# Two attention layers on one core: the first loads of a kernel, dealt differently to two DMA queues

## The chip, the cores and the metric

The kernel runs on one core of a Trainium2 chip. A core has a matrix engine (TensorE, PE in the profile), three engines for element-wise work (VectorE = DVE, ScalarE = ACT, GpSimd = POOL), a queue engine without arithmetic (SyncE = SP) and 16 DMA engines that move data between main memory (HBM) and the core's own memory (SBUF). A load is an instruction on one engine, here SP or ACT; that engine is busy with it while the load is issued ("SPq", "ACTq" in the profile), and the data arrives later ("to landing"). The metric is device time in microseconds (us), the median of several runs.

## The reference

Two independent problems A and B with the same shapes (all bf16) are computed and put side by side:

```python
B, Sq, D = 16, 32, 1024
Hq, Hkv, Sk, Dh = 32, 4, 512, 128
q = (x @ wq).reshape(B, Sq, Hq, Dh).transpose(0, 2, 1, 3)
k = repeat(k_cache, Hq // Hkv, axis=1); v = repeat(v_cache, Hq // Hkv, axis=1)
p = softmax(einsum("bhqd,bhkd->bhqk", q, k) * Dh ** -0.5)
o = einsum("bhqk,bhkd->bhqd", p, v)
out = o.transpose(0, 2, 1, 3).reshape(B, Sq, Hq * Dh) @ wo
result = concatenate([out_A, out_B], axis=-1)
```

For each problem x is 512 tokens by 1024 features, wq is 1024 by 4096 (32 heads of 128 columns), wo is 4096 by 1024.

## The kernel before, in words

Everything runs on one core in an order written out by hand: the function `fast_path` records instructions engine by engine, and each engine executes its own list in that order. Three kinds of TensorE work are woven together in one long loop (from line 613 on): scores and values of the attention, one group of 8 heads and 32 tokens at a time, and between them "units" of the big projections (q = x @ wq, then out = o @ wo), one matmul each. Later loads are tied to slots of that loop.

The change concerns what comes before the loop: the first eight heads of q of problem A (lines 455 to 556). A matmul contracts 128 features, so x and wq are cut along their 1024 features into eight chunks, numbered from 0. For a chunk TensorE needs x transposed (features on the partitions, the tile `xT[0]`) and the rows of wq for that chunk (the tiles `w0`). All of it arrives by loads:

- **x plain**, `load_x` (line 465): columns of chunks 0 and 1 only, in two halves of 256 tokens, called x first half and x second half here, 128 KB each. TensorE transposes them itself (`transpose_x`, line 521), eight 128x128 transposes; VectorE copies chunk 0 from PSUM to `xT[0]`, ScalarE copies chunk 1 (line 525).
- **x transposed by the DMA**, `load_x_transposed` (line 468): two chunks in each call, 256 KB, straight into `xT[0]`. Three calls: chunks 2 and 3 (**T2** here), chunks 4 and 5 (**T4**), chunks 6 and 7 (**T6**).
- **wq**, `load_w0` (line 474): chunk 0 for heads 0 to 2 and for heads 3 to 5 (**W0a**, **W0b**, 96 KB each), chunks 1, 2, 3 for heads 0 to 5 (**W1**, **W2**, **W3**, 192 KB each), then heads 6 and 7 of chunks 0 to 3 together (**WR**, 256 KB), chunk 4 (**W4**, 256 KB), chunks 5 and 6 (**W56**, 512 KB) and chunk 7 (**W7**, 256 KB), each for all eight heads.

TensorE's order in this stage is: 22 warm-up matmuls on a constant (line 513); the eight transposes, first half of the tokens, then second half; chunk 0 for heads 0 to 2 in two halves of 256 columns (six matmuls) and for heads 3 to 5 in full width (three); chunks 1, 2 and 3 for heads 0 to 5 (six matmuls each); heads 6 and 7 for chunks 0 to 3 (eight); chunks 4, 5, 6 for all heads (eight each); chunk 7 (eight). These are the 67 matmuls of line 531 in the profile. Then the units of line 301 follow with the next heads.

ScalarE's list starts with its loads and, after the first of them, the loading of the activation table (line 480), ahead of the two copies of line 525.

One more rule sets the order. The loads issued by SP and ACT share eight semaphores that are handed out in turn. The ninth of these loads may be issued only when the first has landed, the tenth when the second has landed, and so on. In the kernel before, the ninth load is WR and the first is x second half.

Of the kernel before, what the change touches and what calls it, by code (L numbers as in the profile page):

```python
# [181 lines left out]
def kernel(  # L182
# [14 lines left out]
    nc = tc.nc  # L197
# [5 lines left out]
    TT = NTOK // P  # L203
# [14 lines left out]
    def fast_path(ok_i):  # L218
        with ExitStack() as fctx:
# [235 lines left out]
            NF = REP - 2  # L455
# [8 lines left out]
            def load_x(t0, t1, eng=nc.sync):  # L464
                eng.dma_start(out=x_sb[:, t0:t1, :], in_=x_v[:, t0:t1, 0:2 * P])  # L465

            def load_x_transposed(d0):
                nc.sync.dma_start_transpose(  # L468
                    out=xT[0][:, d0:d0 + 2, :],
                    in_=A_x.flatten_outer_dims()[:, d0 * P:(d0 + 2) * P],  # L470
                )

            def load_w0(d0, d1, h0, h1, eng=nc.sync):
                eng.dma_start(  # L474
                    out=w0[d0 // HC][:, d0 % HC:(d1 - 1) % HC + 1, h0 * DH:h1 * DH],
                    in_=wq_v[:, d0:d1, h0 * DH:h1 * DH],
                )

            load_x(TT // 2, TT, nc.scalar)
            nc.scalar.preload_act_table_set("natural_log_exp_and_others")  # L480
            load_x(0, TT // 2)
            load_w0(0, 1, 0, NF // 2)
            load_w0(0, 1, NF // 2, NF, nc.scalar)
            load_w0(1, 2, 0, NF)
            load_w0(2, 3, 0, NF, nc.scalar)
            load_x_transposed(2)
            load_w0(3, 4, 0, NF)
            load_w0(0, HC, NF, REP)
            load_w0(HC, HC + 1, 0, REP)
            load_x_transposed(HC)  # L490
            load_w0(HC + 1, DC - 1, 0, REP)
            load_x_transposed(HC + 2)
            load_w0(DC - 1, DC, 0, REP)
            load_wq(0, 2, 0, 2)
# [173 lines left out]
    ok_i = flag.tile([1, 1], I32, name="ok_i")  # L668
    total = 2 * 2 * NG * QW
    ok = fast_path(ok_i)  # L670
    with tc.If(ok < total, preferred_fallthrough_block=True, label="general"):
        general_path(tc, problems, out_flat)
# [30 lines left out]
```

## Time and profile before

| | |
|---|---|
| time, median of 6 runs | 343.07 us (342.67 to 343.26) |
| the profiled execution | 343.47 us, of which the span of the core 341.7 us |
| busy, share of the span | PE 99%, DVE 78%, ACT 54%, POOL 14% |
| matmuls of line 531 (this stage) | 67, mean 376 ns, 14.6 us busy |
| loads of T2, T4, T6 on SP | 3, 1.57, 1.56 and 3.22 us to issue |

Spans are counted from the first instruction of the core. Matmuls are pipelined: the profile's duration of one (379 ns for 512 columns) is from start to modelled end, and two neighbours overlap; what one costs in a dense row is the distance of the starts. A busy share of 99% thus says that TensorE hardly ever had nothing in flight. DMA share in the table of stretches is the mean busy share of the 16 DMA engines; packets in flight at once on one engine can take it above 1.

### The profile page before, as it was taken

The numbers are of one execution on the slowest core, as the hardware profiler recorded it, in microseconds if no ns is written. First come the engines' busy times: TensorE is split into PE (matmuls) and PEld (weight loads), VectorE is DVE, ScalarE is ACT, GpSimd is POOL, SyncE is SP. The second block draws the span as 40 slices with busy tenths as digits, with TensorE's granted clock in tenths as the row PEclk, the third lists the DMA queues.
The fourth block names the chain that finished last, engine by engine and source line by source line (L and its number), as shares of the span: only waits on it lengthen the run. The fifth ranks groups of instructions, "written<-read, shape, count | busy, mean of one in ns | idle before, by whom it ended". The sixth has DMA issues, their size and how long they took to land.

```text
span 341.7 us, 5475 instructions
## 1 busy us (share of the span) xinstructions
PE 337.0 (99%) x2113; PEld 213.0 (62%) x2113; DVE 265.1 (78%) x335; ACT 185.4 (54%) x208; POOL 46.7 (14%) x206
## 2 busy tenths in 40 slices
PE   8999999999999999999999999999999999999996
PEld 5455666666666666666666666666666666666555
DVE  0046988888888888888888988879888888889540
ACT  2058666676667667666645555555555555555110
POOL 0001110011111111110012211222122101111100
PEclk9999999999999999999999999999999999999999
DMA  7999999999999998899999955998449996440001
GB/s 189 280 207 271 296 239 225 211 235 260 307 257 151 231 223 230 206 288 305 324 276 279 272 125 145 336 283 220 118 103 296 358 204 158 106 100 10 17 19 33
DMA packets 128622, 71.70 MB, mean 210 GB/s; under 512 B 76880, under 2 KB 127824, under 8 KB 128592
## 3 DMA queue, kind: packets, MB, share of 16 engines
q1 hardware_dynamic: 127504, 69.78, 83.7%
q0 software_dynamic: 384, 1.05, 0.8%
q10 hardware_dynamic: 704, 0.49, 0.4%
q8 instruction: 17, 0.28, 0.3%
q14 instruction: 13, 0.11, 0.1%
HBM read 50.59 MB, written 2.10 MB: 154 GB/s over the span
## 4 chain that ended last, share of the span: by engine, by line
PE 96%; DMA 2%; SPq 1%; ACT 0%; issue 0%; ACTq 0%
PE f_ps L320 32%; PE q_ps L301 28%; PE ob L425 16%; PE s_ps L357 16%; PE q_ps L531 3%; DMA w_sb<-in_A_wq_dram 2%; SPq L468 0%; SPq L474 0%; SPq L465 0%; ACT o_sb L329 0%; ACTq L329 0%
## 5 line engine op out<-in xcount | busy, mean ns | idle before, releaser
L365 ACT ACTIVATE p_sb<-s_ps,shift 128x1024 bf16<-128x1024 f32 x128 | 142.7, 1115 | 97.5 <-PE s_ps L357 90.1
L376 DVE TRANSPOSE_TENSOR_REDUCE parts<-p_sb 128x32 f32<-128x1024 bf16 x128 | 158.7, 1240 | 21.0 <-ACT p_sb L365 19.3
L320 PE MATMUL f_ps<-wo_sb,oT 128*128 128x512 bf16 (+1 forms) x544 | 132.3, 366 | 0.0
L301 PE MATMUL q_ps<-xT,wq_sb 128*128 128x512 bf16 x448 | 116.9, 379 | 0.0
L425 PE MATMUL ob<-p_sb,v_sb 128*128 128x256 bf16 x512 | 76.8, 273 | 0.0
L357 PE MATMUL s_ps<-qT,kT 128*128 128x256 bf16 x512 | 76.8, 273 | 0.0
L320 PEld LDWEIGHTS <-oT 128*128 128x128 bf16 x544 | 53.2, 98 | 35.3
L357 PEld LDWEIGHTS <-kT 128*128 128x128 bf16 x512 | 56.9, 113 | 28.3
L301 PEld LDWEIGHTS <-wq_sb 128*128 128x128 bf16 x448 | 43.8, 98 | 32.2
L425 PEld LDWEIGHTS <-v_sb 128*128 128x128 bf16 x512 | 50.1, 98 | 20.0
L447 DVE TENSOR_TENSOR oT<-r,ob 128x512 bf16<-128x512 f32 x64 | 43.9, 686 | 19.9 <-PE ob L425 19.4
L411 DVE STREAM_TRANSPOSE r<-rall 128x512 f32<-128x512 f32 x64 | 44.2, 691 | 1.1
L309 ACT CAST qT<-q_ps 128x512 bf16<-128x512 f32 x56 | 32.7, 583 | 16.5 <-PE q_ps L301 16.5
L394 POOL COPY half<-cs 64x32 f32<-64x32 f32 x32 | 6.5, 204 | 232.3 <-DVE cs L384 232.2
L329 ACT CAST o_sb<-f_ps 128x512 bf16<-128x512 f32 (+1 forms) x17 | 9.5, 559 | 23.6 <-PE f_ps L320 23.6
L531 PE MATMUL q_ps<-xT,w_sb 128*128 128x512 bf16 (+1 forms) x67 | 14.6, 376 | 0.7 <-DMA w_sb<-in_A_wq_dram 0.6
L553 DVE CAST qT<-q_ps 128x512 bf16<-128x512 f32 x4 | 2.5, 684 | 13.7 <-PE q_ps L531 13.7
L384 DVE TENSOR_REDUCE cs<-parts 128x32 f32<-128x128 f32 x32 | 12.1, 377 | 1.1
L406 DVE RECIPROCAL rall<-sums 128x32 f32<-128x32 f32 x32 | 10.2, 319 | 3.3 <-POOL sums L403 3.3
L531 PEld LDWEIGHTS <-w_sb 128*128 128x128 bf16 x67 | 6.6, 101 | 8.3 <-DMA w_sb<-in_A_wq_dram 1.6
L553 ACT CAST qT<-q_ps 128x512 bf16<-128x512 f32 x4 | 2.1, 599 | 13.2 <-PE q_ps L531 13.2
L331 POOL DMA_DIRECT2D out_dram<-o_sb x8 | 4.6, 574 | 29.3 <-ACT o_sb L329 29.3
(25 smaller groups left out, 48.2 us busy)
## 6 DMA issues: line engine op xcount, KB each, us to landing
v_sb<-in_A_v_cache_dram SPq DMA_DIRECT2D x16, 512.0 KB, 5.8
wq_sb<-in_B_wq_dram SPq DMA_DIRECT2D x8, 1024.0 KB, 5.9
wo_sb<-in_A_wo_dram SPq DMA_DIRECT2D x8, 1024.0 KB, 7.5
v_sb<-in_B_v_cache_dram SPq DMA_DIRECT2D x16, 512.0 KB, 4.4
wo_sb<-in_B_wo_dram SPq DMA_DIRECT2D x8, 1024.0 KB, 8.5
wq_sb<-in_A_wq_dram SPq DMA_DIRECT2D x5, 1024.0 KB, 6.7
wq_sb<-in_A_wq_dram SPq DMA_DIRECT2D x2, 512.0 KB, 6.7
kT<-in_A_k_cache_dram SPq DMA_TRANSPOSE x64, 4.4
```

The lines of the kernel that those rows point to most:

```text
L301: nc.tensor.matmul(ps[:], lhsT=w[:, dc, (h % 4) * DH:(h % 4 + 1) * DH], rhs=xT[pr][:, dc, :], start=(dc == 0), stop=(dc == DC - 1),)
L309: nc.scalar.copy(out=qT[pr, g][:, :, hl, :], in_=ps[:].rearrange("p (b s) -> p b s", s=SQ),)
L320: nc.tensor.matmul(ps[:, 0:width], lhsT=oT[pr, tt][:, h, :], rhs=wo_tiles[pr, nh, h // REP][:, h % REP, off:off + width], start=(h == 0), ...
L357: nc.tensor.matmul(s_ps[:, c, :], lhsT=kT[:, i % GRP, c, :], rhs=qT[pr, g][:, b, :, :].rearrange("p h s -> p (h s)"), start=True, stop=True,)
L365: nc.scalar.activation(out=p_sb[:], in_=s_ps[:], func=ACTF.Exp, bias=shift[:], scale=SCALE)
L376: nc.vector.tensor_reduce(out=parts[k][:, q, :, :].rearrange("p c h -> p (c h)"), in_=st[i]["p"][:].rearrange("p c (h s) -> p (c h) s", s=SQ),
L384: nc.vector.tensor_reduce(out=cs[:], in_=parts.pop(k)[:].rearrange("p q c h -> p q h c"), axis=AX.X, op=ALU.add,)
L406: nc.vector.reciprocal(out=rall[:, k, :], in_=quad.pop(k)[:])
L411: nc.vector.transpose(out=r[:].rearrange("p n s -> p (n s)"), in_=rall[:, k, o * 2 * REP:(o + 1) * 2 * REP] .unsqueeze(2).to_broadcast([P, ...
L425: nc.tensor.matmul(ob[j][:, q, :], lhsT=v_sb[:, i % GRP, c, :], rhs=st[i]["p"][:, c, :], start=(c == 0), stop=(c == KC - 1),)
L447: nc.vector.tensor_tensor(out=out, in0=rcp.pop(j)[:].rearrange("p (q h) s -> p q h s", h=REP), in1=ob.pop(j)[:].rearrange("p q (h s) -> p ...
L531: nc.tensor.matmul(first_q[h][:, ts], lhsT=w0[dc // HC][:, dc % HC, h * DH:(h + 1) * DH], rhs=xT[0][:, dc, ts], start=(dc == 0 and t0 == 0 ...
```

## The change

T2 goes from SP's list to ACT's, and to the very front of it; it is ACT's only load at the start. The three loads that ACT issued before (x second half, W0b, W2) go to SP. SP's order is now x first half, x second half, W0a, W0b, W1, W2, W3, WR, W4, T4, W56, T6, W7; in the kernel before it was x first half, W0a, W1, T2, W3, WR, W4, T4, W56, T6, W7. What is loaded, in what pieces and into which tiles stays, and so does the work of every other engine. The ninth load is again WR; the first, whose landing it waits for, is now T2.

```diff
-            def load_x_transposed(d0):
-                nc.sync.dma_start_transpose(
+            def load_x_transposed(d0, eng=nc.sync):
+                eng.dma_start_transpose(
                     out=xT[0][:, d0:d0 + 2, :],
                     in_=A_x.flatten_outer_dims()[:, d0 * P:(d0 + 2) * P],
                 )
...
-            load_x(TT // 2, TT, nc.scalar)
+            load_x_transposed(2, nc.scalar)
             nc.scalar.preload_act_table_set("natural_log_exp_and_others")
             load_x(0, TT // 2)
+            load_x(TT // 2, TT)
             load_w0(0, 1, 0, NF // 2)
-            load_w0(0, 1, NF // 2, NF, nc.scalar)
+            load_w0(0, 1, NF // 2, NF)
             load_w0(1, 2, 0, NF)
-            load_w0(2, 3, 0, NF, nc.scalar)
-            load_x_transposed(2)
+            load_w0(2, 3, 0, NF)
             load_w0(3, 4, 0, NF)
             load_w0(0, HC, NF, REP)
             load_w0(HC, HC + 1, 0, REP)
```

## The prediction

> **What bounds the kernel now.** I read the chain of work that ended last, then TensorE's own waits, then TensorE's rows at the start.
>
> ```profile
> PE 96%; DMA 2%; SPq 1%; ACT 0%; issue 0%; ACTq 0%
> PE q_ps L513 <- PEq L687: 0.9, 1, 0.9
> PE q_ps L531 <- DMA w_sb<-in_A_wq_dram: 0.6, 1, 0.6
> ```
>
> The chain is TensorE nearly throughout, and TensorE waited for only two things: the program's start and one load of wq. Behind the first stage it is never idle, so what this stage gains or loses reaches the end one for one.
>
> ```profile
> 3.37 1.06 PE L521 MATMUL xT_ps<-ident,x_sb 128*128 128x128 bf16 x8
> 4.22 0.81 PE L531 MATMUL q_ps<-xT,w_sb 128*128 128x256 bf16 x3
> 5.62 0.38 PE L531 MATMUL q_ps<-xT,w_sb 128*128 128x512 bf16 x1
> 6.55 0.82 PE L531 MATMUL q_ps<-xT,w_sb 128*128 128x512 bf16 x3 [0.55 <-DMA w_sb<-in_A_wq_dram]
> 8.94 3.90 PE L531 MATMUL q_ps<-xT,w_sb 128*128 128x512 bf16 x16
> 19.36 3.62 PE L301 MATMUL q_ps<-xT,wq_sb 128*128 128x512 bf16 x16
> 22.81 0.60 PE L357 MATMUL s_ps<-qT,kT 128*128 128x256 bf16 x4
> ```
>
> The pace of a dense row is (22.81 - 19.36) / 16 = 0.216 us for 512 columns. The last matmul of chunk 0 starts at 5.62, so chunk 1 could start at 5.835; it starts at 6.55, when W1 is there: **0.72 us lost**. The last matmul of chunk 2 starts at 8.94, chunk 3 could follow at 9.15; the chain has W3 landing at 9.38 and chunk 3 from 9.42: **0.27 us lost**. Together 0.99 us, all that this stage loses to late loads of wq.
>
> ```profile
> 3.84 5.54 DMA w_sb<-in_A_wq_dram
> 9.42 10.10 PE q_ps L531 x46
> ```
>
> Why W3 needs 5.5 us where W0a needed 2.8 is seen in the stretches; the last two columns are the DMA engines' busy share and GB/s:
>
> ```profile
> 3.00:3.50 0.50, 0.50 (x7) 0.32 (x5) 0.00 (x0) 0.00 (x0) 0.00 (x0) 1.00 1.06 346
> 5.00:5.50 0.50, 0.50 (x6) 0.36 (x4) 0.00 (x0) 0.00 (x0) 0.00 (x0) 1.00 1.60 278
> 5.50:6.00 0.50, 0.50 (x3) 0.00 (x1) 0.00 (x0) 0.00 (x0) 0.00 (x0) 1.00 1.34 120
> 6.00:6.50 0.50, 0.00 (x0) 0.00 (x0) 0.00 (x0) 0.00 (x0) 0.00 (x0) 1.00 0.62 86
> ```
>
> Between 5.5 and 6.5 the engines are occupied and move about 100 GB/s. That is where T2 (issued 2.22, landing 7.6) is in flight, with W3 behind it in SP's queue and W1 and W2 still running on two queues. The same sag (57 and 20 GB/s) comes at 9.5 to 10.5, when T4 is in flight. [...]
>
> **The change part by part.**
>
> SP's issues. Removed: T2, 1.57 us. Added: x second half (0.46 on ACT), W0b and W2 (0.45 each), 1.36 us. With some 0.05 us between issues SP reaches x first half at 0.74 as before, x second half at 1.25 (ACT had it at 0.82), W0a at 1.75 (1.25), W0b at 2.24 (ACT 1.34), W1 at 2.74 (1.75), W2 at 3.22 (ACT 1.83), W3 at 3.72 (3.84), WR at about 4.3 (4.46).
>
> ACT. T2 is issued at 0.82 instead of 2.22. Taken at SP's 1.57 us it ends at 2.4; the table load (1.28) then ends at 3.7, before the copies of line 525, which started at 4.01. Cost nothing; the cover is 0.3 us. Should the issue take T6's 3.22 us, table and two copies (0.82) end at 6.15, still before 6.55.
>
> x second half. It landed at 0.82 + 3.0 = 3.82. The load issued at 1.25 before, W0a, took 2.8: low end 4.05, 0.23 late. High end: all of T2 passes first; 256 KB at the 250 GB/s or so of the stretches from 2.0 on are 1.0 us: 5.05. T2's first data cannot come much earlier than x's own, so I take a share of a quarter, **4.3**. Transposes and copy took 0.40 to the first matmul of chunk 0 (3.82 to 4.22): chunk 0 starts at 4.7, 0.48 late. W0a at 1.75 + 2.8 = 4.55 is in time; W0b at 2.24 + 2.9 = 5.1 is needed 0.4 to 0.6 after the start, in time or 0.1 late. Three matmuls of 256 columns took 0.213 each at the start (4.22 to 4.86), the next three 0.109: TensorE doubles its pace at about 4.85. A later start puts two of the three behind that point, which returns 0.21. Chunk 0 ends 0.27 late, at **6.10**.
>
> W1. By bytes: x, T2, W0 and W1 are 896 KB; from 2.0 to 5.0 the trace moved 256 GB/s, so 3.6 us from the first data at about 1.75, and some 0.5 to the semaphore: 5.85, inside 6.10. The low end is 2.74 + 2.8 = 5.5, the high end its old 4.8 us, 7.5. I take the bytes, since the 4.8 contains the sag. Chunk 1 starts at 6.10: **0.45 gained** (ends: 0.7 gained, 0.95 lost).
>
> T2 and W3. Chunk 2 needs T2 at 6.10 + 1.30 = 7.4. T2's landing lies between 4.7 us (the first half of problem B's x, 512 KB, in a calmer stretch) and 6.4 (T4, T6): 5.5 to 7.2. In time. W3, with no transposing load ahead of it in its queue, lands by bytes (1280 KB at 256 GB/s) at 7.4, needed at 8.7: **0.27 gained** (ends 0 and 0.27).
>
> SP's ninth load. WR now waits for T2, so SP stands from 4.3 to about 5.5, and WR, W4, T4, W56, T6, W7 and the wq and K loads behind them are issued 1.1 us later. WR is needed at 6.10 + 18 x 0.216 = 10.0 and lands by 5.5 + 4.3: covered, at the rate of W7. T4 would be issued at 6.6, is needed at 11.72, and took 6.4 with the long queue of before, 4.7 with a short one: 11.3 to 13.0. I take it as just in time, because W1 to W3 are through by then. Ends: 0, or 1.3 lost. Behind it, the next wq half landed at 17.2 against a need at 19.4, covered.
>
> Sum: 0.45 + 0.27 = **0.72 us**. The profiled execution (343.47, span 341.7) would become 342.75; it lies 0.40 over the median of 343.07, so the forecast is **342.35**.
>
> [...] The trace shows SP's and ACT's first issues overlapping (0.74 and 0.82) at 0.45 and 0.46 us, no longer than alone. [...]
>
> **The rivals.**
>
> A. *Early loads late.* T2 and x share the DMA engines from the first packet, and T2 holds x second half and W0 back by the full 1.0 us. For it: the sags whenever a transposing load meets others. Against: T2 now meets little unfinished work. Chunk 0 starts at 5.45, ends at 6.75 (1.30 at full pace): 0.20 lost, 0.27 gained, 343.0. Between 342.8 and 343.4.
>
> B. *SP's new wait.* WR behind T2, then T4 late, at chunk 4. For it: T4 landed at 11.9 against a need at 12.45, only 0.57 to spare. Against: the shorter queue. At T4's old 6.4 us it lands at 13.0: 1.3 lost minus 0.72, 343.6. It turns to a net loss once T4 lands after 12.45.
>
> C. *The pace* (the one clearly slower). TensorE's doubling at 4.85 followed unbroken work since 0.93. With x late it stands empty for some 0.5 us between 3.24 and 4.7. If the wait of 3.9 us (0.93 to 4.85) began anew at 4.3, the doubling would come at 8.2: 3.35 us at half pace cost 1.68, minus 0.72, 344.0. It decides when the doubling is over 1.44 us late. Against: the gap of 0.72 us at 5.84 did not slow the matmuls after it. [...]
>
> **How the numbers follow.** Likeliest case 0.55, own range 341.95 to 342.75; A 0.22; B 0.11; C 0.12. 0.2% is 0.69 us, about what a measurement of this kernel tells from no change; the likeliest case sits on that line. Faster: 0.40 + 0.02 + 0.01 = 0.43. Same: 0.15 + 0.17 + 0.03 = 0.35. Slower: 0.03 + 0.07 + 0.12 = 0.22. The range reaches from all 0.99 us gained and a little noise (342.0) to most of B and half of C, 343.8.
>
> **What would show it.** Right: chunk 1 starting at 5.9 to 6.3, chunk 3 without a wait, no sag before 7 us, an unbroken row from there. Wrong: first transposes of the second half after 4.6 (A), a wait of line 531 at chunk 4 (B), 0.43 us between starts of 512-column matmuls after 5 us (C).

## The result, and the profile after

The changed kernel takes **344.90 us** (median of 20 runs, 343.03 to 345.78) against 343.17 (40 runs, 342.67 to 343.62): **0.44% slower, ratio 1.0044 with a 95% interval of 1.0034 to 1.0055**. The ratio weighs all runs; the medians lie 0.50% apart. It was forecast at 342.35.

The median hides the shape. The runs of the changed kernel fall into two groups: 5 of 20 between 343.03 and 343.25, 15 between 344.44 and 345.78, none in between. The kernel before has one group, 0.95 us wide. The profiled execution belongs to the short group: 343.24 us, span 341.3. First the chain by engine and TensorE's waits in it:

```profile
PE 98%; DMA 1%; SPq 0%; ACT 0%; issue 0%; ACTq 0%
PE q_ps L513 <- PEq L687: 0.9, 1, 0.9
PE xT_ps L521 <- DMA x_sb<-in_A_x_dram: 0.6, 1, 0.6
```

The wait for wq in line 531 has gone, as forecast; a new one stands in its place, in the transposes of line 521, for the second half of x. The timeline of the same execution:

```profile
0.82 1.35 ACTq L468 DMA_TRANSPOSE xT<-in_A_x_dram  x1
3.24 0.63 PE L521 MATMUL xT_ps<-ident,x_sb 128*128 128x128 bf16 x4
4.47 0.44 PE L521 MATMUL xT_ps<-ident,x_sb 128*128 128x128 bf16 x4 [0.60 <-DMA x_sb<-in_A_x_dram]
5.05 14.12 PE L531 MATMUL q_ps<-xT,w_sb 128*128 128x256 bf16 x67
19.01 3.62 PE L301 MATMUL q_ps<-xT,wq_sb 128*128 128x512 bf16 x16
```

The first four transposes are through at 3.67, the other four begin at 4.47: TensorE is empty for 0.80 us by starts. From 5.05 on all 67 matmuls follow without a wait worth naming, and line 301 starts at 19.01, 0.35 us earlier than before. So this execution gained, half of what was forecast. The chain runs through W0a, which lands at 5.00:

```profile
1.75 3.25 DMA w_sb<-in_A_wq_dram
```

The landings of the first loads (KB, us from issue) and the stretches (last three columns: granted clock, DMA share, GB/s):

```profile
x_sb<-in_A_x_dram SPq DMA_DIRECT2D x1, 128.0 KB, 2.4
x_sb<-in_A_x_dram SPq DMA_DIRECT2D x1, 128.0 KB, 3.2
xT<-in_A_x_dram ACTq DMA_TRANSPOSE x1, 3.9
...
4.00:4.50 0.50, 0.03 (x1) 0.03 (x2) 0.00 (x0) 0.28 (x1) 0.00 (x0) 1.00 1.35 211
5.50:6.00 0.50, 0.50 (x5) 0.21 (x3) 0.00 (x0) 0.00 (x0) 0.00 (x0) 1.00 1.04 323
6.00:6.50 0.50, 0.50 (x4) 0.20 (x3) 0.00 (x0) 0.00 (x0) 0.00 (x0) 1.00 0.91 314
```

The sag at 5.5 to 6.5 (120 and 86 GB/s before) is gone, the engines move over 300 GB/s there. T2 lands at 4.7 instead of 7.6. The second half of x lands at 4.45 instead of 3.82. None of this explains 344.9; a profile of a long execution does.

### The profile page after: what moved, and what is told of

Its sections match the earlier page's. It is cut to its first block, busy times and chain, and to the rows that moved or that the text cites. A ratio compares the mean times of both kernels' runs of the same rounds, so it can differ in the third digit from the quotient of the medians.

```text
span 341.3 us, 5475 instructions
## 1 busy us (share of the span) xinstructions
PE 336.6 (99%) x2113; PEld 212.8 (62%) x2113; DVE 265.1 (78%) x335; ACT 185.2 (54%) x208; POOL 46.6 (14%) x206
## 4 chain that ended last, share of the span: by engine, by line
PE 98%; DMA 1%; SPq 0%; ACT 0%; issue 0%; ACTq 0%
PE f_ps L320 32%; PE q_ps L301 28%; PE s_ps L357 16%; PE ob L425 16%; PE q_ps L531 4%; DMA w_sb<-in_A_wq_dram 1%; SPq L465 0%; ACT o_sb L329 0%; ACTq L329 0%
```

## The experiments

Two theories stood against each other. **P (pace):** TensorE starts at half pace and doubles it after a stretch of work (256-column matmuls start 0.213 us apart up to 4.86 in the profile of the kernel before, then 0.109); an empty stretch in the first 5 us puts the doubling off. **L (loads):** in long executions loads come still later than in the profile at hand, and TensorE waits for them.

In the table each ratio is to runs of the kernel before from the same series and weighs all runs; it is not the quotient of two medians.

| run | time, us (runs) | ratio to before, 95% interval |
|---|---|---|
| after_again | 345.22 (4; 344.80 to 345.66) | 1.0065 (1.0050 to 1.0079) |
| fill | 343.30 (11; 343.00 to 344.12) | 1.0009 (1.0000 to 1.0018) |
| fill16 | 343.78 (11; 343.05 to 344.61) | 1.0018 (1.0008 to 1.0027) |
| before_w14 | 343.45 (10; 342.72 to 344.83) | 1.0012 (1.0001 to 1.0024) |
| before_x2late | 346.57 (4; 345.99 to 347.38) | 1.0093 (1.0078 to 1.0109) |
| t2_on_sp | 343.63 (10; 343.16 to 344.08) | 1.0014 (1.0005 to 1.0023) |
| x2_then_t2 | 343.83 (12; 343.11 to 346.15) | 1.0035 (1.0018 to 1.0051) |
| table_then_t2 | 344.93 (12; 343.26 to 345.65) | 1.0044 (1.0028 to 1.0061) |
| w3_then_t2 | 343.73 (11; 343.31 to 344.25) | 1.0016 (1.0007 to 1.0025) |
| before_again | 342.57 (1) | |

### The changed kernel again: a long execution

No edit. (The expectation counts 14 long and 6 short runs; of the 20 runs it is 15 and 5.)

> The changed kernel once more, to see an execution of the longer kind (344.4 to 345.8 us, 14 of 20 runs; the other 6 were 343.0 to 343.3). Theory P (pace): TensorE has nothing to do for about 0.8 us before the second half of x lands, and in most executions its pace then doubles some 3 us later than at 4.6; a profile of a long execution shows starts of 512-column matmuls 0.43 us apart after 5 us, no added wait on loads, and a span of 342.5 to 344. Theory L (loads): in a long execution the pace doubles at 4.6 to 4.9 as in the profile at hand, and TensorE waits 1.2 to 2.5 us for W0, W1, T2 or T4. Times in both theories: two groups, near 343.2 and 345.0.

The profile caught a long execution: 345.09 us, span 343.3. Its stretches, matmuls of line 531 alone (PE busy and in brackets how many matmuls were under way at some time in the stretch, the same for weight loads, granted clock, DMA share, GB/s), after the row of the transposes; the last row is of the short execution:

```profile
4.59 0.60 PE L521 MATMUL xT_ps<-ident,x_sb 128*128 128x128 bf16 x4 [0.72 <-DMA x_sb<-in_A_x_dram]
5.10 8.27 PE L531 MATMUL q_ps<-xT,w_sb 128*128 128x256 bf16 x31
...
6.00:7.00 1.00, 1.00 (x5) 0.54 (x4) 1.00 0.71 209
7.00:8.00 1.00, 1.00 (x3) 0.30 (x2) 1.00 0.93 278
8.00:9.00 1.00, 1.00 (x4) 0.39 (x3) 1.00 1.38 265
9.00:10.00 1.00, 1.00 (x6) 0.39 (x5) 1.00 0.91 182
...
7.00:8.00 1.00, 1.00 (x6) 0.41 (x5) 1.00 0.85 269
```

The second half of x is late by 0.12 us more than in the short execution, and chunk 0 starts at 5.10 against 5.05: the loads are all but the same, TensorE is busy without a break, and line 531 waits for nothing. But from 7 to 9 only three or four matmuls are under way in a microsecond, where the short execution has six. Single starts of 512-column matmuls lie 0.427 us apart until 9.32 and 0.216 after. In the short execution the doubling comes at 4.6. Half pace from 5.10 to 9.32 loses 4.22 / 2 = 2.1 us; the spans differ by 2.0. Theory P has its mechanism and its size, L has neither.

### The gap filled

The changed kernel with eight more warm-up matmuls between the two halves of x:

```diff
                 transpose_x(0, *ts, nc.vector.tensor_copy)
                 transpose_x(1, *ts, nc.scalar.copy, spare[k])
+                if k == 0:
+                    warm_up(8)
```

> The changed kernel with eight more warm-up matmuls on the constant between the transposes of the first and of the second half of x, which fill the 0.8 us in which TensorE was empty; no load is touched. Theory P: the long executions go away, all runs at 342.7 to 343.3, median about 343.0 (0.1 to 0.5 under the kernel before). Theory L: the two groups stay, median about 344.9.

No run above 344.12; the median falls from 344.9 to 343.30. No load was touched, so the long group is made by the empty TensorE. In the profiled execution the second half of x was later still:

```profile
3.67 1.06 PE L513 MATMUL q_ps<-const-bfloat16-1.0 128*128 128x128 bf16 x8
5.13 0.61 PE L521 MATMUL xT_ps<-ident,x_sb 128*128 128x128 bf16 x4 [0.40 <-DMA x_sb<-in_A_x_dram]
```

Even so the pace doubled at 6.19. This is no faster than the kernel before, though: five of eleven runs lie over the 343.3 that was expected at most, and the gain of 0.1 to 0.5 us is not there.

With 16 warm-ups in place of 8 the gap is closed altogether:

> The changed kernel with 16 instead of 8 warm-up matmuls between the two halves of x: they last until about 5.4 at half pace, past the latest landing of the second half seen (5.13). Theory P (an empty TensorE in the first 5 us delays the doubling of its pace): no run over 344; the doubling at 4.4 to 7.8 in the profile; median 343.2 to 343.6, since the longer filling can itself hold up the transposes by up to 0.9 us. Theory L (late loads alone make the long runs): long runs of 345 stay.

The median is 343.78: the filling itself lasts until 5.38 and holds up the transposes, as expected; the second half of x had landed at 4.9. But three of eleven runs lie over 344, which theory P had ruled out, and two of them, 344.48 and 344.61, reach the lower end of the long group. The one profile (343.78, all starts at full pace from 5.95 on) does not show what these runs spent their time on, so this form supports P less clearly than `fill` does.

### A gap in the kernel before

```diff
-            warm_up(22)
+            warm_up(14)
```

> The kernel before with 14 warm-up matmuls in place of 22: TensorE is empty from about 2.4 to 3.36 us, 0.9 us, in the same first 4.5 us; no load is touched. Theory P: long executions appear in the kernel before too, runs between 343 and 345.5, median 0.5 to 2 us over the kernel before. Theory L: nothing changes, 343.2 within 0.3.

A miss in size. One run of ten is long (344.83), the median rises by 0.12% only. TensorE was empty from 2.39 to 3.10 and its pace doubled at 7.0, as P has it, but here the half pace ran while W1 was on its way in any case: chunk 0, at half pace, ends at 6.50 and chunk 1 follows at once, where the first profile of the kernel before has chunk 1 waiting until 6.55. So the late doubling cost little here: a load was the limit.

The second form, again of the kernel before, makes the gap where the changed kernel has it:

```diff
-            load_x(TT // 2, TT, nc.scalar)
             nc.scalar.preload_act_table_set("natural_log_exp_and_others")
...
             load_w0(2, 3, 0, NF, nc.scalar)
+            load_x(TT // 2, TT, nc.scalar)
```

> The kernel before with one swap in ScalarE's queue: the second half of x goes behind W0b and W2, so it is issued at about 1.8 instead of 0.82; T2 stays where it was. It lands at 4.6 to 5.0, TensorE is empty from 3.67 on for 0.9 to 1.3 us, with T2 untouched. Theory P: long runs of 344.5 to 346 appear beside runs near 343.3, median over 343.8; in a long run 512-column matmuls start 0.43 us apart after 6 us. Theory L, in the form that the early T2 makes the long runs: no long runs, median 343.2 to 343.6.

```profile
6.34 0.61 PE L521 MATMUL xT_ps<-ident,x_sb 128*128 128x128 bf16 x4 [2.05 <-DMA x_sb<-in_A_x_dram]
...
9.00:10.00 1.00, 1.00 (x4) 0.33 (x3) 1.00 1.25 321
10.00:11.00 1.00, 1.00 (x3) 0.30 (x2) 1.00 1.03 389
```

T2 is where it was, and all four runs are long, 346.57. The second half of x lands even later than expected (1.75 + 4.54 = 6.29), so part of the 3.4 us is the empty stretch itself, which is longer here than in the changed kernel (2.05 us against 0.60 in the rows); the other part is the pace, which doubles at 12.26 in the profile.

### What makes the second half of x late

The other half of the change alone: all loads on SyncE, T2 at its old place (the edit is to the changed kernel, as in the two forms after it).

```diff
-            load_x_transposed(2, nc.scalar)
...
             load_w0(2, 3, 0, NF)
+            load_x_transposed(2)
             load_w0(3, 4, 0, NF)
```

> The other half of the change alone: all loads on SyncE, but T2 at its old place, between W2 and W3; ScalarE issues no load at the start. The second half of x is issued at 1.25 as in the changed kernel. If the early T2 makes the second half late (A), it lands at 3.6 to 3.9 here, TensorE is empty for 0.3 us at most, there are no long runs, and the time is 343.0 to 343.8 with the wait for W1 back. If the later place in the queue makes it late, it lands at 4.3 to 4.6 and long runs appear as in the changed kernel.

```profile
x_sb<-in_A_x_dram SPq DMA_DIRECT2D x1, 128.0 KB, 2.2
w_sb<-in_A_wq_dram SPq DMA_DIRECT2D x1, 96.0 KB, 2.2
...
3.24 1.06 PE L521 MATMUL xT_ps<-ident,x_sb 128*128 128x128 bf16 x8
4.10 1.62 PE L531 MATMUL q_ps<-xT,w_sb 128*128 128x256 bf16 x9
```

Issued at 1.25 as in the changed kernel, the second half lands in 2.2 us, at 3.45, and W0a at 1.75 + 2.2 = 3.95; with T2 in ScalarE's queue they took 3.2 and 3.25. All eight transposes run without a break, and no run is above 344.08. So, by one profile of this form, it is the early T2, not the later place in the queue, that costs the second half of x a microsecond. The place in the queue costs next to nothing: 3.45, against 3.82 and 3.32 in the two profiles of the kernel before. The rest is not better than before: T2 in SyncE's queue brings back waits at chunks 1, 2 and 3: chunk 1 starts at 5.97, behind 0.25 us of idle time, and chunk 3 at 9.12 instead of 5.97 + 12 x 0.216 = 8.56, 0.56 us lost at chunks 2 and 3 together.

Putting the second half of x ahead of T2 in ScalarE's queue moves the delay to the loads behind it:

```diff
+            load_x(TT // 2, TT, nc.scalar)
             load_x_transposed(2, nc.scalar)
             nc.scalar.preload_act_table_set("natural_log_exp_and_others")
             load_x(0, TT // 2)
-            load_x(TT // 2, TT)
```

> The changed kernel with the second half of x put back to the front of ScalarE's queue; T2 follows it there, all loads of wq stay on SyncE. The second half lands at 3.8 to 4.1 instead of 4.45, so TensorE is empty for 0.2 us at most before it. Theory P: no long executions; chunk 1 starts at 5.9 to 6.2, no wait at chunk 3; median 342.4 to 342.9. Theory L: as the loads of wq still share the queue with T2, two groups stay, median over 344.

The second half landed at 0.82 + 2.6 = 3.42, as wanted, but then W0a came at 4.8 and W0b at 7.17, and five of twelve runs lie between 345.06 and 346.15, where theory P, which did not reckon with a late W0a, had expected no long run. The profiled execution (346.15) shows the pace in the granted clock. Timeline rows, then stretches of all instructions:

```profile
4.83 0.83 PE L531 MATMUL q_ps<-xT,w_sb 128*128 128x256 bf16 x6 [0.73 <-DMA w_sb<-in_A_wq_dram]
7.18 6.16 PE L531 MATMUL q_ps<-xT,w_sb 128*128 128x512 bf16 x20 [1.51 <-DMA w_sb<-in_A_wq_dram]
...
6.50:7.00 0.50, 0.00 (x0) 0.00 (x0) 0.00 (x0) 0.00 (x0) 0.00 (x0) 1.00 0.80 160
7.00:7.50 0.50, 0.32 (x1) 0.13 (x2) 0.00 (x0) 0.00 (x0) 0.00 (x0) 0.67 1.09 366
7.50:8.00 0.50, 0.50 (x2) 0.15 (x1) 0.00 (x0) 0.00 (x0) 0.00 (x0) 0.50 1.06 368
10.00:10.50 0.50, 0.50 (x2) 0.15 (x1) 0.00 (x0) 0.00 (x0) 0.00 (x0) 0.50 1.26 287
10.50:11.00 0.50, 0.50 (x3) 0.21 (x2) 0.00 (x0) 0.00 (x0) 0.00 (x0) 0.92 1.04 329
```

TensorE doubled its pace at 3.77, then stood empty for most of 3.94 to 7.18, fell back to half pace at 7.18 and doubled again at 10.57. The three moments are 3.41 and 3.39 us apart.

Exchanging the table load and T2 on ScalarE was meant to start T2 later:

```diff
-            load_x_transposed(2, nc.scalar)
             nc.scalar.preload_act_table_set("natural_log_exp_and_others")
+            load_x_transposed(2, nc.scalar)
```

> The changed kernel with two lines exchanged: ScalarE loads its activation table first and issues T2 after it, at about 2.1 instead of 0.82; SyncE's order stays. Theory P with A (the early T2 makes the second half of x late, the empty TensorE then delays the doubling of its pace): the second half lands near 3.5 as with T2 on SyncE, TensorE has no gap before chunk 0, no long runs near 345; T2 lands at 6.0 to 6.8, in time for chunk 2; WR, which waits for T2, is issued at 6.0 to 6.8, and T4 two loads later may now come after its need at 11.7 (rival B): 342.6 to 343.8, median about 343.2. If the loads on one queue make the second half late whatever T2 does: two groups with a median over 344.

It did not move T2, so it could not answer its question; it is the changed kernel once more, with the same two groups (344.93; in the profile the second half of x at 5.14):

```profile
0.82 1.28 ACT L479 ACT_TABLE_LOAD   x1 [0.82 <-PEq L687]
0.85 1.35 ACTq L468 DMA_TRANSPOSE xT<-in_A_x_dram  x1
```

### The stall of the kernel before

In the kernel before, W3 was put ahead of T2 in SyncE's queue:

```diff
-            load_x_transposed(2)
             load_w0(3, 4, 0, NF)
+            load_x_transposed(2)
```

> The kernel before with T2 and W3 exchanged in SyncE's queue: W3 no longer stands behind a transposing load, T2 is issued at 2.8 instead of 2.2. If T2 among unfinished loads holds up W1 and W3 (the sag at 5.5 to 6.5), W3 lands by 7.5 and W1 by 5.9 to 6.5, and T2 becomes the last, at 7.6 to 8.2 against a need at 7.2 to 7.8: 0 to 0.7 us gained, 342.4 to 343.2, no long runs. If W1 is late for another reason, chunk 1 starts at 6.5 as before and T2 late: 343.2 to 343.8.

```profile
2.69 5.43 DMA xT<-in_A_x_dram
8.16 4.04 PE L531 MATMUL q_ps<-xT,w_sb 128*128 128x512 bf16 x18 [0.67 <-DMA xT<-in_A_x_dram]
```

W1 came at 6.0 and W3 in time, but T2 landed at 8.12 and chunk 2 waited 0.84 us for it (7.11 + 0.216 to 8.16): 343.73, over the 342.4 to 343.2 expected for a W1 that comes in time. The wait was only handed on.

> The kernel before once more, for a second profile of it: the one at hand took 343.47, above the median of 343.17. If the waits at chunk 1 and chunk 3 (0.72 and 0.27 us) belong to an execution slower than most, they sum to 0.5 to 0.8 us here, at a span near 341.4; if they are the rule, to 0.9 to 1.1 us.

```profile
4.10 1.57 PE L531 MATMUL q_ps<-xT,w_sb 128*128 128x256 bf16 x9
5.83 6.43 PE L531 MATMUL q_ps<-xT,w_sb 128*128 128x512 bf16 x29 [0.16 <-DMA w_sb<-in_A_wq_dram]
```

This execution took 342.57 us, span 340.7. Chunk 1 could start at 5.51 and starts at 5.83, 0.32 us lost; at chunk 3 nothing is lost. That is less than the 0.5 to 0.8 expected, but this execution is also one of the shortest. The 0.99 us of the first profile belongs to one of the longest (343.47 us; only 3 of the 40 runs were longer). By these two profiles less was to be won in most; a profile of a median execution is not on record.

## Why the prediction was wrong

**The bound** held: TensorE is the chain nearly throughout, and what the first stage loses is in the time one for one (4.22 / 2 = 2.1 us at half pace, 2.0 us in the span).

**SP's and ACT's issues** came as worked out for the first loads (1.25, 1.75), later up to 0.2 us late (W1 2.95 against 2.74). T2 took 1.35 us on ACT, and the table load behind it ended at 3.48, before the first copy at 3.91: no cost. SP's issue of x second half, from 1.25 to 1.70 beside T2's from 0.82 to 2.17, took the same 0.45 us as without T2 in `t2_on_sp`, so T2 did not hold back the issue.

**The second half of x** was put at 4.3; 4.45, 4.55 and 5.14 were measured in the profiles of `after`, `after_again` and `table_then_t2`. The share of a quarter for T2 was too small: without T2 beside it the load took 2.2 us, with T2 3.2 to 3.9. **W0a** was called in time at 4.55; it landed at 5.00, and W0b at 5.78 instead of 5.1, 0.1 late. These terms were taken from a run in which T2 was issued only after them. Chunk 0 therefore ended at 6.49 instead of 6.10, and the gain at chunk 1 was 0.06 us instead of 0.45. This is the mechanism of rival A, inside the likeliest case.

**W1, W3, T2**: there is no wait at chunks 1 to 3, the sag is gone, T2 came at 4.7 (forecast 5.5 to 7.2) and W3 at 7.5 (7.4). W1 was put at 5.85 and landed at 6.29. No wait shows only because chunk 0 ended late: had it ended at 6.10, chunk 1 would have had to wait for W1. W1 took 3.3 us from its issue instead of 4.8, but it was issued 1.2 us later; in the second profile of the kernel before it landed at 5.8. So the 0.45 us at chunk 1 was too large even without the late x.

**SP's ninth load**: WR was issued at 4.71 instead of 5.5, because T2 landed sooner; T4 was never late. Rival B did not occur in any profile of the changed kernel.

**The step that failed** is the one on the pace: "TensorE doubles its pace at about 4.85. A later start puts two of the three behind that point, which returns 0.21." The doubling was treated as a fixed moment. It came near that with TensorE kept busy (4.86 and 4.3 in the two profiles of the kernel before). The late second half of x leaves TensorE empty for 0.8 us or more before the doubling, and, by the two groups of times, that puts the doubling off in 15 of 20 runs. In the profiled long execution it came at 9.32: 2.0 us more. This is rival C. It had been named, with a price of 1.0 us net (a doubling at 8.2 against a full gain of 0.72) and a chance of 0.12. The price was too low, as the doubling came later and only half the gain was there. And the case was set aside for a wrong reason: the gap of 0.72 us at 5.84 that left the pace alone lay behind the doubling, and the gap here lay before it. (It was also the shorter one, 0.72 us against 0.80 and 0.92 in the two profiles of the changed kernel; no run shows by itself which of the two differences counts.)

The chain of causes is shown link by link: T2 in front makes the second half of x late (t2_on_sp against the changed kernel, 2.2 against 3.2 us); the gap makes the long executions (fill removes them with the loads untouched, before_x2late makes them, by a longer gap, with T2 untouched); and in a long execution the time goes into half pace and not into waits (after_again).

**The base** was an execution 0.4 us over the median. The difference was carried over to the forecast as a constant; by the two profiles of the kernel before it was part of the very wait that the change removes (0.99 us in that one, 0.32 in the other). This fits the short group of the changed kernel, 343.03 to 343.25, which is no faster than the kernel before (median 343.17).

## What to carry to other kernels

A load that delays the first real operand by a microsecond can cost two, through the pace: here 1.0 us later for x second half, 2.1 us at half pace. Warm-up work that left no long break before that operand protected the pace (`fill`, 343.30 against 344.90, no run over 344.12), but where it outlasted the operand's landing it cost time itself (`fill16`, 343.78 against 343.30). A transposing load at the very front slowed the plain loads beside it, though issued by another engine (2.2 us to landing became 3.2 to 3.9); with x second half alone ahead of it, the wait passed to W0a and W0b. No order tried here was faster than the kernel before. And where a kernel's times spread, take a second profile before a stall is put into a sum: the one at hand may show the stall at its largest.

## What was not expected of the hardware

**When the pace changes.** TensorE's idle time in the rows before the transposes of the second half of x (in `before_w14` of the first), and the moment of the doubling, each from one profile:

| run | idle, us | pace doubles at, us |
|---|---|---|
| kernel before, first profile | 0 | 4.86 |
| before_again | 0 | 4.3 |
| x2_then_t2 | 0 | 3.77 |
| fill | 0.40 | 6.19 |
| before_w14 | 0.51 | 7.0 |
| changed kernel, short execution | 0.60 | 4.6 |
| after_again, long execution | 0.72 | 9.32 |
| before_x2late | 2.05 | 12.26 |

Where nothing was idle the doubling came by 4.86. But the length of the idle time alone does not give the moment: 0.51 us goes with 7.0, 0.60 with 4.6. What else sets it was not shown. The two groups of times of one kernel go with the two moments 4.6 and 9.32; the idle time of the two executions differs too (0.60 and 0.72), and no run separates its length from the moment at which it falls. Once the pace was lost again: in x2_then_t2 it fell back at 7.18, after TensorE had been busy for 0.94 of the 3.00 us from 4.00 to 7.00, and doubled again at 10.57.

**The granted clock did not show the first half pace.** It reads 1.00 in the long execution while 512-column matmuls start 0.427 us apart, and 0.50 for the same pace in x2_then_t2, after a doubling had been lost. In these profiles the first half pace is read from the distance of the starts.

**Issuing beside a table load.** A load behind the activation table load in ScalarE's list was issued at 0.85, while the table load ran from 0.82 to 2.10.
